# Odd high halves cast on VectorE instead of by DMA, and all squares on ScalarE

## The chip, the cores and the metric

The kernel runs on one core of one Trainium2 chip. The time is device microseconds of one execution; the kernel before took 1809.41 us (median of 3 runs, 1804.36 to 1811.67). Names used below: PE is TensorE's matmul side and PEld its weight loads, ACT is ScalarE, DVE is VectorE, POOL is GpSimd, SP is the sync engine, which here only issues DMAs.

## What is computed

An attention through 49 agents per batch, followed by a two-layer network with a squared ReLU between the layers:

```python
def _attn_ref(q, k, v, agents):
    scale = 1.0 / np.sqrt(q.shape[-1])
    def sm(a, b):
        s = scale * (a @ b.transpose(0, 2, 1))
        s = s - s.max(-1, keepdims=True)
        e = np.exp(s)
        return e / (e.sum(-1, keepdims=True) + 1e-09)
    agent_v = sm(agents, k) @ v
    return sm(q, agents) @ agent_v

def _moe_ref(x, w_in, w_out):
    h = x @ w_in
    r = np.maximum(h, 0.0)
    g = r * r
    return g @ w_out
```

There are 4 batches of 12480 rows with 128 channels; the network goes from 128 to 2048 hidden channels and back. All inputs are fp32.

## The kernel before

**Groups.** The 49920 rows are cut into 52 sets of 960 rows, and the 2048 hidden channels into 16 slices of 128. A set and a slice make a *group* i, from 0 to 831 (16 groups a set); g, gh, gl below are tiles of 128 hidden channels by 960 rows of one group. A group goes through these steps, in this order:

1. `mm1` on PE (L414): three pairs of matmuls give h in PSUM. The weights are agent values times w_in, and both operands are split in a rounded and a rest part (p_a, p_b, w_a, w_b). h has two buffers, so `mm1(i+2)` waits until `relu(i)` has read its h.
2. `relu` on ACT (L418), g from h.
3. `square` of g in place, on ACT (L424), or on DVE (L422) where `by_vector(i)` says so: from group 32 on, every fifth group (i % 5 == 3), 159 of 832.
4. `high`: gh, the rounded half of g, in the type that matmuls read at full rate. By a DMA from SBUF to SBUF that POOL issues (L429) for all groups but the last four, which DVE casts (L431).
5. `low` on DVE (L435): gl = g - gh, the rest.
6. `mm2` on PE (L453): two neighbouring groups j (even) and j+1 are taken together, gh of both with wo_hi and wo_lo, then gl of both with wo_hi. Within one call the order is: gh(j) with wo_hi, gh(j) with wo_lo, gh(j+1) with wo_hi, gh(j+1) with wo_lo, gl(j), gl(j+1). There are two calls for a pair, which differ in the halves of the PE array that the banks use.

**Order.** Every engine runs its instructions in the order in which the program issues them. The program collects all steps with a due time (`at(t, step)`), in units of one group, and sorts by it. `mm1(i)` is due at i, `relu(i)` at i + .1, `square(i)` at i + 1.2 (1.3 on DVE), `high(i)` at i + 3.05 by DMA and i + 2.35 on DVE, `low(i)` at i + 5.9 for even and i + 5.3 for odd groups with a DMA, i + 4.3 without one. The two `mm2` calls of the pair j, j+1 are due at j + 8 and j + 9 (LAG is 8). Due times set only the order; when a step runs is decided by its waits.

**Relay.** Between the two `mm2` calls of a pair the array's halves change places. A nop on POOL (L447) then waits for the matmuls before, and the matmuls after wait for the nop. So this nop stands in POOL's queue among the DMAs of `high`.

**Attention.** The work of the attention is put between the groups: scores of queries and keys on PE (L167), sums over values (L230), products for w_a and w_b (L310); exponentials on ACT (L209 for keys, L356 for queries), copies L182 and L319; maxima, sums, transposes and the store's copy (L469) on DVE. Its loads of kT, qT and v and the stores are issued by SP.

**Buffers.** g has 10, gh 9 and gl 7 buffers.

Of the kernel before, what the change touches and what calls it, by code (L numbers as in the profile page):

```python
# [13 lines left out]
AF = mybir.ActivationFunctionType  # L14
ALU = mybir.AluOpType
# [12 lines left out]
def agent_attention_relu2_kernel(ctx: ExitStack, tc: tile.TileContext, qT, kT, v, agT, w_in, w_out, outT):  # L28
# [6 lines left out]
    nc = tc.nc  # L35
# [4 lines left out]
    NF = F // P  # L40
    NSG = qT.shape[1] // ST
    NS = NSG // B
    NG = NSG * NF
# [350 lines left out]
    hs, gs, ghs, gls = {}, {}, {}, {}  # L394
# [23 lines left out]
        nc.scalar.activation(gs[i], hs.pop(i)[:, :, :TT], AF.Relu)  # L418

    def square(i):  # L420
        if by_vector(i):
            nc.vector.tensor_tensor(gs[i], gs[i], gs[i], op=ALU.mult)  # L422
        else:
            nc.scalar.activation(gs[i], gs[i], AF.Square)  # L424

    def high(i):
        ghs[i] = ew.tile([P, 2, TT], F32R, name="gh", bufs=HB)
        if by_dma(i):
            nc.gpsimd.dma_start(out=ghs[i], in_=gs[i])  # L429
        else:  # L430
            nc.vector.tensor_copy(ghs[i], gs[i])  # L431
# [47 lines left out]
    SKIP = (7, 12)  # L479

    def by_dma(i):
        return i < NG - 4

    def by_vector(i):
        return i >= 2 * NF and i % 5 == 3 and by_dma(i)

    steps = []

    def at(t, f, *args):
        steps.append((t, len(steps), f, args))  # L490
# [8 lines left out]
    def chain(t, todo):  # L499

        first = prev = None
        while todo:
            n = 1
            while todo[0][0] == "PE" and n < len(todo) and (todo[n][1] in reads_bank and todo[n][0] != "PE" or todo[n][1:-1] == todo[n - 1][1:-1] and todo[n][1] is not k_bias):
                n += 1
            t += hop[prev][todo[0][0]] if prev else 0
            while True:
                g, p, ts = t, None, []  # L510
                for e, f, *_ in todo[:n]:
                    g += hop[p][e] if p else 0
                    while (e, g) in taken:
                        g += 1
                    ts.append(g)
                    p = e
                held = range(ts[0], ts[-1] + (4 if todo[0][1] is v_acc else 2 if todo[0][1] is w_make else 3)) if todo[0][0] == "PE" else ()
                if not any(y in banks for y in held):
                    break
                t += 1  # L520
            banks.update(held)
            for (e, f, *args), g in zip(todo, ts):
                taken.add((e, g))
                at(g + (.005 + .015 * args[2] if f is w_make and args[2] < 2 else .5), f, *args)
            first = ts[0] if first is None else first
            prev, t, todo = p, ts[-1], todo[n:]
        return first, t
# [26 lines left out]
    def plan_keys(b, n, t):  # L554

        first, end = chain(t, [("PE", k_scores, b, n), ("ACT", k_copy, n), ("DVE", k_max, n)])
        for x in range(2):
            if b > 1 or n > 1:
                at(first - LEAD + .1 * x, k_load, b, 2 * n + x)
        print('K', b, n, first, end)  # L560
        return end

    def plan_bias(t):
        _, end = chain(t, [("DVE", k_bias, 0), ("PE", k_bias, 1), ("DVE", k_bias, 2), ("PE", k_bias, 3), ("DVE", k_bias, 4)])
        return end

    def plan_values(b, t0, stop):

        used, turned = {}, {}
        d = (stop - TAIL - t0) / NP  # L570
        for n in range(NP):
            _, t1 = turned[n] = chain(max(t0 + 1 + int(n * d), used.get(n - 2, 0)), [("ACT", k_exp, n), ("DVE", k_turn, n)])
            print('V', b, n, t1)
            used[n], end = chain(t1 + 3, [("PE", v_acc, n), ("DVE", v_sum, n)])
            for x in range(2):
                at(used[n] - LEAD + .1 * x, v_load, b, 2 * n + x)
        print('Vend', b, end, stop)
        last, end = chain(end + 2, [("PE", a_final, 0), ("DVE", a_final, 1), ("DVE", a_final, 2)])
        assert end < stop - 6, (b, end, stop)
        if b < B - 1:  # L580
            for n in range(NP):
                keys = plan_keys(b + 1, n, turned[n][1] + 5)
            return max(last + 2, plan_bias(keys + 1))
# [96 lines left out]
    for b in range(1, B):  # L680
        for f, x in enumerate((-6, -3, 0, 4)):
            first, end = chain(b * NS * NF + x, [("PE", w_make, b, f, 0), ("PX", w_make, b, f, 1), ("ACT", w_make, b, f, 2), ("DVE", w_make, b, f, 3)])
# [3 lines left out]
    end = 19  # L686
    for n in range(NP):
        end = plan_keys(1, n, end + 3)
    ready = plan_bias(end + 1)
    for b in range(1, B):  # L690
        ready = plan_values(b, ready, b * NS * NF)

    for i in range(NG):
        late = i in SKIP or i < NF + LAG and (i < LAG or (i - LAG) % NF == 0)
        at(i if late else i + .01, mm1, i)
        at(i + .1, relu, i)
        at(i + (1.3 if by_vector(i) else 1.2), square, i)
        if by_dma(i):
            at(i + 3.05, high, i)
            at(i + (5.3 if i % 2 else 5.9), low, i)  # L700
        else:
            at(i + 2.35, high, i)
            at(i + 4.3, low, i)
# [52 lines left out]
```

## Time and profile before

| | before |
|---|---|
| median of 3 runs | 1809.41 us |
| the profiled execution | 1806.67 us |
| its span, first to last instruction | 1804.9 us |
| busy: PE, DVE, ACT, POOL | 1748.7, 1449.7, 1471.4, 477.7 us |
| DMA queues: packets' share of 16 engines, software and hardware queue | 68.7% and 21.3% |
| moved by the 828 DMAs gh<-g, 480 KB each | 4.7 us median from issue to landing |

The span is 1.8 us shorter than the time of the same execution. A matmul's end in the profile is modelled, and neighbouring matmuls overlap, so a busy share of 97% for PE doesn't mean that the array lost only 3%. Of the waits, only what stands between two instructions of one engine is shown, with the event that ended it.

### The profile page before, as it was taken

The numbers are of one execution on the slowest core, as the hardware profiler recorded it, in microseconds if no ns is written. First come the engines' busy times: TensorE is split into PE (matmuls) and PEld (weight loads), VectorE is DVE, ScalarE is ACT, GpSimd is POOL, SyncE is SP. The second block draws the span as 40 slices with busy tenths as digits, with TensorE's granted clock in tenths as the row PEclk, the third lists the DMA queues.
The fourth block names the chain that finished last, engine by engine and source line by source line (L and its number), as shares of the span: only waits on it lengthen the run. The fifth ranks groups of instructions, "written<-read, shape, count | busy, mean of one in ns | idle before, by whom it ended". The sixth has DMA issues, their size and how long they took to land.

```text
span 1804.9 us, 41518 instructions
## 1 busy us (share of the span) xinstructions
PE 1748.7 (97%) x16831; PEld 1493.8 (83%) x16835; DVE 1449.7 (80%) x1509; ACT 1471.4 (82%) x1645; POOL 477.7 (26%) x897
## 2 busy tenths in 40 slices
PE   8899999999999999999999999999999999999998
PEld 4578787888887887888888888888898898889897
DVE  6978777787886886787887787887888789788886
ACT  4788877887887887888888788887898898889886
POOL 0322222222222222222222222222232222223231
PEclk9999999999999999999999999999999999999999
DMA  9799998999989989989979889989998998999885
GB/s 375 263 302 350 302 275 305 308 318 318 304 271 347 293 292 311 316 283 336 306 274 306 262 308 320 303 277 307 297 294 277 299 307 294 303 302 305 289 303 193
DMA packets 169664, 541.42 MB, mean 300 GB/s; under 512 B 21806, under 2 KB 34368, under 8 KB 169472
## 3 DMA queue, kind: packets, MB, share of 16 engines
q0 software_dynamic: 127136, 419.18, 68.7%
q1 hardware_dynamic: 42336, 119.59, 21.3%
q8 instruction: 132, 2.16, 0.5%
q14 instruction: 60, 0.49, 0.1%
HBM read 81.47 MB, written 25.56 MB: 59 GB/s over the span
## 4 chain that ended last, share of the span: by engine, by line
PE 68%; DMA 17%; issue 6%; DVE 4%; ACT 3%; POOL 0%; SPq 0%; POOLq 0%; DVEq 0%; ACTq 0%
PE out L453 41%; PE h L414 20%; DMA gh<-g 16%; PE ps_att L167 4%; ACT g L424 3%; DVE gl L435 3%; PE ps_att L230 1%; DMA kt<-kT 1%; PE ps_att L310 1%; PE out L230 0%; ACT g L418 0%; DVE g L422 0%; DVE cv_x L88 0%; POOL wo_lo L113 0%; PE h L167 0%
## 5 line engine op out<-in xcount | busy, mean ns | idle before, releaser
L435 DVE TENSOR_TENSOR gl<-g,gh 128x960 fp32r<-128x960 f32 x832 | 934.3, 1149 | 242.1 <-DMA gh<-g 208.8
L418 ACT ACTIVATE g<-h 128x960 f32<-128x960 f32 x832 | 807.7, 971 | 286.2 <-PE h L414 282.9
L429 POOL DMA_DIRECT2D gh<-g x828 | 439.5, 531 | 1243.3 <-ACT g L424 724.5
L424 ACT ACTIVATE g<-g 128x960 f32<-128x960 f32 x673 | 670.7, 997 | 0.0
L453 PE MATMUL out<-gh,wo_hi 64*128 64x480 f32 x3328 | 627.5, 373 | 25.5 <-DMA gh<-g 16.7
L453 PE MATMUL out<-gh,wo_lo 64*128 64x480 f32 x3328 | 610.4, 363 | 0.0
L453 PE MATMUL out<-gl,wo_hi 64*128 64x480 f32 x3328 | 490.8, 368 | 15.7 <-DVE gl L435 15.2
L453 PEld LDWEIGHTS out<-gh,wo_hi 64*128 64x128 f32 x3328 | 314.3, 185 | 106.7 <-issue 38.9
L453 PEld LDWEIGHTS out<-gl,wo_hi 64*128 64x128 f32 x3328 | 316.8, 187 | 57.4 <-DVE gl L435 35.4
L453 PEld LDWEIGHTS out<-gh,wo_lo 64*128 64x128 f32 x3328 | 317.5, 187 | 21.2
L414 PE MATMUL h<-p_a,w_a 49*128 49x480 f32 x1664 | 311.5, 371 | 0.5 <-ACT w_a L294 0.4
L414 PE MATMUL h<-p_a,w_b 49*128 49x480 f32 x1664 | 305.4, 363 | 0.0
L414 PE MATMUL h<-p_b,w_a 49*128 49x480 f32 x1664 | 304.9, 363 | 0.0
L422 DVE TENSOR_TENSOR g<-g 128x960 f32<-128x960 f32 x159 | 183.0, 1151 | 29.2 <-ACT g L418 28.2
L414 PEld LDWEIGHTS h<-p_a,w_a 49*128 49x128 f32 x1664 | 158.9, 187 | 15.4 <-ACT g L418 2.9
L414 PEld LDWEIGHTS h<-p_b,w_a 49*128 49x128 f32 x1664 | 160.4, 189 | 10.9
L414 PEld LDWEIGHTS h<-p_a,w_b 49*128 49x128 f32 x1664 | 157.0, 185 | 12.8
L469 DVE COPY ob<-out 128x960 f32<-128x960 f32 x51 | 58.7, 1151 | 14.5 <-PE out L453 14.2
L167 PE MATMUL ps_att<-qt,ag_sb 128*32 128x480 f32 x408 | 47.2, 572 | 0.7 <-DVE w_b L321 0.7
L344 DVE STREAM_TRANSPOSE e<-ps_att 128x960 f32<-128x960 f32 (+1 forms) x26 | 30.7, 1179 | 10.8 <-PE ps_att L167 10.5
L230 PE MATMUL ps_att<-vt,pe 128*49 128x129 f32 x588 | 36.7, 275 | 0.0
L230 PEld LDWEIGHTS ps_att<-vt,pe 128*49 128x49 f32 x588 | 31.4, 123 | 6.4 <-issue 5.2
(95 smaller groups left out, 596.8 us busy)
## 6 DMA issues: line engine op xcount, KB each, us to landing
gh<-g POOLq DMA_DIRECT2D x828, 480.0 KB, 4.7
vt<-v SPq DMA_DIRECT2D x56, 451.5 KB, 9.0
kt<-kT SPq DMA_DIRECT2D x56, 448.0 KB, 8.3
qt<-qT SPq DMA_DIRECT2D x52, 480.0 KB, 7.0
outT<-ob SPq DMA_DIRECT2D x51, 480.0 KB, 5.2
pt<-et SPq DMA_DIRECT2D x204, 60.0 KB, 5.8
p_a<-pt POOLq DMA_DIRECT2D x50, 211.9 KB, 3.8
raw<-w_in SPq DMA_DIRECT2D x4, 512.0 KB, 10.7
```

The lines of the kernel that those rows point to most:

```text
L167: nc.tensor.matmul(ps[32 * j:32 * j + 32, h, :w], ags[j // 2][:, 32 * h:32 * h + 32], xs[j // 2][:, j % 2 * w:j % 2 * w + w], start=True, ...
L230: nc.tensor.matmul(ps[t:t + A, :C + 1], pes[n][:, c, :A], vt[:, y, :], start=n == first and c < 2, stop=n == last and c >= KC - 2)
L310: mm = nc.tensor.matmul(ps[:M, u, :256], av2[rows], win_sb[rows, f * 512 + u * 256:f * 512 + u * 256 + 256], start=step == 0, stop=step == 1)
L344: nc.vector.transpose(squares(es[u]), pss.pop(("q", u))[r, :, :TT].rearrange("p h (b c) -> p h b c", c=32))
L414: nc.tensor.matmul(hs[i][:, t, :TT], w, two(p), start=n == 0, stop=n == 2)
L418: nc.scalar.activation(gs[i], hs.pop(i)[:, :, :TT], AF.Relu)
L422: nc.vector.tensor_tensor(gs[i], gs[i], gs[i], op=ALU.mult)
L424: nc.scalar.activation(gs[i], gs[i], AF.Square)
L429: nc.gpsimd.dma_start(out=ghs[i], in_=gs[i])
L435: nc.vector.tensor_tensor(out=gls[i], in0=gs.pop(i), in1=ghs[i].bitcast(F32), op=ALU.subtract)
L453: mm = nc.tensor.matmul(o[:, u, :TT], w[rows, j, :], two(g[rows, u, :]), start=first and n == 0, stop=last and n == len(todo) - 1)
L469: nc.vector.tensor_copy(ob, o[:, :, :TT])
```

## The change

From group 48 on (the fourth set of 16), odd groups no longer get gh by DMA: DVE casts them, due at i + 2.35, and their `low` is due at i + 4.3. That is 390 of the 828 DMAs. Even groups keep the DMA. `by_vector` goes, so that the 159 squares of DVE run on ACT, due at i + 1.2. Two lines that only print are dropped.

```diff
     def square(i):
-        if by_vector(i):
-            nc.vector.tensor_tensor(gs[i], gs[i], gs[i], op=ALU.mult)
-        else:
-            nc.scalar.activation(gs[i], gs[i], AF.Square)
+        nc.scalar.activation(gs[i], gs[i], AF.Square)
...
     def by_dma(i):
-        return i < NG - 4
-
-    def by_vector(i):
-        return i >= 2 * NF and i % 5 == 3 and by_dma(i)
+        return i < NG - 4 and (i % 2 == 0 or i < 3 * NF)
...
         at(i + .1, relu, i)
-        at(i + (1.3 if by_vector(i) else 1.2), square, i)
+        at(i + 1.2, square, i)
         if by_dma(i):
             at(i + 3.05, high, i)
             at(i + (5.3 if i % 2 else 5.9), low, i)
```

(In the lines below these, `else` gives a group without a DMA its cast at i + 2.35 and its `low` at i + 4.3, as before.) Line numbers of `high`, `low`, `mm2` and `store` are smaller by 3 after the change, and `square` is L421.

DVE's queue before, at groups 98 to 103. Here g_3456 belongs to group 98, g_3483 to 99, g_3509 to 100, g_3547 to 101, g_3573 to 102 and g_3606 to 103:

```order
L435 TENSOR_TENSOR gl_3615<-g_3456,gh_3545 128x960
L435 TENSOR_TENSOR gl_3641<-g_3483,gh_3571 128x960
L422 TENSOR_TENSOR g_3606<-g_3606 128x960
L352 TENSOR_TENSOR e_3523<-e_3523,mx_3578 128x15x49
L435 TENSOR_TENSOR gl_3672<-g_3509,gh_3602 128x960
L435 TENSOR_TENSOR gl_3698<-g_3547,gh_3637 128x960
L391 TENSOR_TENSOR p_b_3610<-pt_3239,p_a_3609 113x480
L213 STREAM_TRANSPOSE pe_3730<-sk_87 128x2x14x32
L435 TENSOR_TENSOR gl_3732<-g_3573,gh_3664 128x960
```

The same place after it. Here g_3458 belongs to group 98, g_3483 to 99, g_3511 to 100, g_3547 to 101, g_3606 to 103 and g_3666 to 105:

```order
L432 TENSOR_TENSOR gl_3609<-g_3483,gh_3552 128x960
L428 CAST gh_3611<-g_3547 128x960
L466 COPY ob_3616<-out_3122 128x960
L432 TENSOR_TENSOR gl_3619<-g_3458,gh_3545 128x960
L432 TENSOR_TENSOR gl_3669<-g_3547,gh_3611 128x960
L428 CAST gh_3671<-g_3606 128x960
L352 TENSOR_TENSOR e_3523<-e_3523,mx_3578 128x15x49
L432 TENSOR_TENSOR gl_3676<-g_3511,gh_3602 128x960
L391 TENSOR_TENSOR p_b_3614<-pt_3243,p_a_3613 113x480
L432 TENSOR_TENSOR gl_3730<-g_3606,gh_3671 128x960
L428 CAST gh_3732<-g_3666 128x960
L213 STREAM_TRANSPOSE pe_3734<-sk_87 128x2x14x32
```

The subtraction of an odd group (101) has moved ahead of that of its even neighbour (100), a cast of the next odd group stands behind each of them, and the square of group 103 is gone from this queue.

ACT's queue before, at the square that DVE has (group 98, g_3456):

```order
L418 ACTIVATE g_3456<-h_3447 128x960
L424 ACTIVATE g_3430<-g_3430 128x960
L418 ACTIVATE g_3483<-h_3474 128x960
L418 ACTIVATE g_3509<-h_3500 128x960
L424 ACTIVATE g_3483<-g_3483 128x960
```

And after it (group 98 is g_3458):

```order
L418 ACTIVATE g_3458<-h_3451 128x960
L421 ACTIVATE g_3430<-g_3430 128x960
L418 ACTIVATE g_3483<-h_3474 128x960
L421 ACTIVATE g_3458<-g_3458 128x960
L418 ACTIVATE g_3511<-h_3504 128x960
L421 ACTIVATE g_3483<-g_3483 128x960
```

Before, two ReLUs stood side by side in every fifth group; now a square stands between any two of them. In both, the square of a group comes behind the ReLU of the next one.

## Rows read from the trace of the kernel before

**Rows 1.** The page: busy time of each engine, share of the span, instructions.
```profile
PE 1748.7 (97%) x16831; PEld 1493.8 (83%) x16835; DVE 1449.7 (80%) x1509; ACT 1471.4 (82%) x1645; POOL 477.7 (26%) x897
```
**Rows 2.** The page: costliest groups (busy us, mean ns of one, idle before, releaser).
```profile
L418 ACT ACTIVATE g<-h 128x960 f32<-128x960 f32 x832 | 807.7, 971 | 286.2 <-PE h L414 282.9
...
L424 ACT ACTIVATE g<-g 128x960 f32<-128x960 f32 x673 | 670.7, 997 | 0.0
...
L422 DVE TENSOR_TENSOR g<-g 128x960 f32<-128x960 f32 x159 | 183.0, 1151 | 29.2 <-ACT g L418 28.2
```
**Rows 3.** The page: the chain that ended last, by engine.
```profile
PE 68%; DMA 17%; issue 6%; DVE 4%; ACT 3%; POOL 0%; SPq 0%; POOLq 0%; DVEq 0%; ACTq 0%
```
**Rows 4.** Waits of PE from 160 to 1786 us: us in total, times, longest.
```profile
PE out L453 <- DMA gh<-g: 16.7, 19, 2.5
PE out L453 <- DVE gl L435: 12.0, 33, 0.5
PE out L453 <- POOLq L447: 5.6, 12, 0.5
```
**Rows 5.** Waits of DVE and of ACT, the same stretch.
```profile
DVE gl L435 <- DMA gh<-g: 201.6, 170, 4.2
DVE g L422 <- ACT g L418: 27.5, 31, 2.5
...
ACT g L418 <- PE h L414: 269.1, 252, 4.1
```
**Rows 6.** Timeline, 286 to 302 us: start, length, instruction, [idle before it, releaser].
```profile
287.83 1.53 SPq L175 DMA_DIRECT2D kt<-kT  x2
...
289.47 1.35 SPq L219 DMA_DIRECT2D vt<-v  x2
...
294.13 0.36 PE L453 MATMUL out<-gh,wo_lo 64*128 64x480 f32 x2
...
296.10 1.16 DVE L435 TENSOR_TENSOR gl<-g,gh 128x960 fp32r<-128x960 f32 x1 [3.63 <-DMA gh<-g]
296.12 0.47 PE L453 MATMUL out<-gh,wo_hi 64*128 64x480 f32 x2 [1.63 <-DMA gh<-g]
```
**Rows 7.** Clock: the whole span, and windows behind stalls (PEclk stands ahead of DMA share).
```profile
core 0: 1804.9 us, clock 0.992
...
297.50:301.00 3.50, 3.50 (x20) 2.96 (x20) 2.51 (x3) 1.95 (x3) 0.53 (x1) 0.52 1.10 408
1024.00:1031.00 7.00, 6.60 (x36) 5.11 (x38) 6.99 (x7) 2.03 (x3) 1.59 (x3) 0.55 0.66 213
```
**Rows 8.** Window 160 to 1786 us: busy time of each engine, clock, DMA share, GB/s.
```profile
160.00:1786.00 1626.00, 1591.24 (x15442) 1384.87 (x15440) 1316.32 (x1345) 1352.67 (x1503) 440.21 (x830) 0.99 0.91 300
```
**Rows 9.** Timeline of ACT behind an exponential, and of ACT and PE undisturbed.
```profile
902.17 0.95 ACT L418 ACTIVATE g<-h 128x960 f32<-128x960 f32 x1
...
903.91 0.96 ACT L418 ACTIVATE g<-h 128x960 f32<-128x960 f32 x1
...
908.51 0.37 PE L414 MATMUL h<-p_a,w_a 49*128 49x480 f32 x2
...
909.33 0.97 ACT L418 ACTIVATE g<-h 128x960 f32<-128x960 f32 x1 [0.86 <-PE h L414]
...
910.34 0.37 PE L414 MATMUL h<-p_a,w_a 49*128 49x480 f32 x2
```
**Rows 10.** The four casts of the tail, by line; tile gh, issue to landing of its DMAs.
```profile
L431 DVE CAST gh<-g 128x960 fp32r<-128x960 f32 x4 | 2.6, 654 | 1.2 <-ACT g L424 1.2
...
DMA to landing us min/median/max: 2.8/4.7/10.8
```
**Rows 11.** Attention's exponentials on ACT, 160 to 1786 us, by line.
```profile
L209 ACT ACTIVATE sk<-sk,mb 128x448 f32<-128x448 f32 x42 | 25.5, 658 | 0.0
L356 ACT ACTIVATE e<-e 128x735 f32<-128x735 f32 (+1 forms) x23 | 18.9, 822 | 0.0
```
**Rows 12.** Tile gh, POOL's issues (ns min/median/max); timeline at 80 us, POOL and DVE.
```profile
L429 POOL DMA_DIRECT2D gh<-g x828: 527/530/1085, 56.4 to 1785.6; - x166
...
80.60 1.60 POOL L429 DMA_DIRECT2D gh<-g  x2
80.76 0.45 DVE L85 TENSOR_SCALAR cv_p<-sk 128x512 uint32<-128x512 uint32 x1
81.10 0.47 DVE L87 TENSOR_SCALAR cv_x<-sk 128x512 uint32<-128x512 uint32 x1
```

More of the change, by code (lines that the diff above doesn't have):

```diff
@@ L559, in plan_keys @@
                 at(first - LEAD + .1 * x, k_load, b, 2 * n + x)
-        print('K', b, n, first, end)
         return end
@@ L572, in plan_values @@
             _, t1 = turned[n] = chain(max(t0 + 1 + int(n * d), used.get(n - 2, 0)), [("ACT", k_exp, n), ("DVE", k_turn, n)])
-            print('V', b, n, t1)
             used[n], end = chain(t1 + 3, [("PE", v_acc, n), ("DVE", v_sum, n)])
@@ L576, in plan_values @@
                 at(used[n] - LEAD + .1 * x, v_load, b, 2 * n + x)
-        print('Vend', b, end, stop)
         last, end = chain(end + 2, [("PE", a_final, 0), ("DVE", a_final, 1), ("DVE", a_final, 2)])
```

## The prediction

> **What bounds the kernel now.** The share of busy time comes first: PE is busy for 97% of the span, ACT for 82%, DVE for 80% [rows 1]. So PE is the engine to feed, and the most that a change to the other engines can give back is PE's stalls. The chain that ended last runs through PE for 68% and through DMA for 17% [rows 3], which says that the DMA of gh often arrives last, not that 17% can be saved. The waits of PE tell how much: from 160 to 1786 us it idles 16.7 us for the DMA of gh (19 times), 12.0 us for gl from DVE (33 times) and 5.6 us for the relay nop on POOL (12 times), 34.3 us in all [rows 4]. Since a matmul's end is modelled, a stall is a little longer than its idle time. A unit (one group) undisturbed takes 910.34 - 908.51 = 1.83 us [rows 9] for nine pairs of matmuls, 0.20 us each; in the stall at 296 us the starts are 1.99 us apart, 1.79 us more than 0.20, where the row says 1.63 [rows 6]. That is 0.15 us more per stall.
>
> That stall also shows the mechanism. The matmul that waits is gh with wo_hi right behind gh with wo_lo, so it is the second, odd group of the pair. Four big loads (two kt, two vt) were issued 5 to 8 us before and share the DMA engines, which are 91% busy [rows 6, 8]. The DMA of gh takes 4.7 us in the median, but 2.8 at best and 10.8 at worst [rows 10]. DVE had then stood for 3.63 us for the same DMA [rows 6]; over the stretch it stands 201.6 us that way [rows 5]. Behind the worst stalls PE's granted clock falls to its lower level, 1.2 GHz: 0.52 and 0.55 of full speed in two such windows [rows 7].
>
> **What is removed.** Four terms, against the profiled execution's 1806.67 us.
>
> Waits for gh: 16.7 + 19 x 0.15 = 19.6 us. The odd group's gh now comes from a cast that is due 4.65 units (8.5 us) before `mm2` needs it, and the even group's DMA runs in a queue that lost 390 of 828 transfers. I take all of it: 19.6.
>
> Waits for gl: 12.0 + 33 x 0.15 = 17.0 us. Gl is late because DVE was held by a DMA, or because DVE is simply behind. The first cause falls away for odd groups and becomes rarer for even ones; the second stays. I take two thirds: 11.3.
>
> Waits for the relay: 5.6 + 12 x 0.15 = 7.4 us. The nop stands in POOL's queue right behind the DMA of an odd group, which waits for that group's square. With odd groups gone, the DMA ahead of the nop is an even one, due two units before it instead of one. I take 7.4.
>
> Clock: 0.008 of the span is missing from full speed [rows 7], 14.4 us, a part of it at the start and the end. I take 10 us as the stalls' share and 8 as what goes with them.
>
> Sum: 46 us.
>
> **What is added, and what hides it.** On DVE, 390 casts at the tail's 654 ns [rows 10] are 255 us, and 159 squares at 1151 ns less [rows 2] are 183 us: 72 us more work, 1522 us, 84% of the span. DVE has 310 us idle in the stretch, 201.6 of it waits for the DMA of gh [rows 5, 8]; the work fits if these waits shrink. On the path I count nothing: within a pair DVE does a cast and two subtractions, and the gl that is done last is due more than 2 units before its matmul. If that cover is gone, every further wait of DVE is gl late at PE.
>
> A cast puts a wait in DVE's queue: for the square on ACT. Behind it are queued the subtraction of the even group and everything of the attention. The nearest row is the square on DVE that goes away, which waited for ACT in the same way: 27.5 us for 156 of them in the stretch [rows 5], 0.18 us each; the four casts of the tail waited 1.2 us together, 0.3 each [rows 10]. So 70 to 117 us for 390 casts, below the 201.6 us of DMA waits that they replace in part. I take nothing on the path, between a gain of some us (DVE is freer) and the loss under the second rival.
>
> On ACT, 159 squares at 997 ns [rows 2] are 159 us: 1630 us busy, 90% of the span. Idle time that it takes: 269.1 us of waiting for h [rows 5]. Undisturbed, ACT waits for PE in every unit; behind an exponential, two ReLUs start 1.74 us apart [rows 9], against PE's 1.83. So ACT keeps pace with squares in every unit but makes up only 0.09 us per unit. A ReLU starts 0.82 us after its `mm1` and lasts 0.97 [rows 9]; `mm1` two units on, 3.65 us later, needs it, so ACT may be 1.8 us late at no cost. An exponential of keys (two of 0.66) makes it 1.3 us late, one of queries 0.8 [rows 11]; both together pass the limit, and attention work on PE gives the time back. Bounds: nothing, and all exponentials of the stretch, 25.5 + 18.9 = 44 us [rows 11]. Most should be absorbed: I take 8.
>
> On POOL, 390 issues of 0.53 us go. Casts and issues can meet: one issue of 828 took 1.085 us instead of 0.53, while two one-input operations of DVE ran, of the kind that the cast is [rows 12]. That bounds the price at 0 and 0.55 us per DMA; an even group's DMA has more than that before DVE needs it, so I take nothing.
> The Trainium skill is harsher here (SBUF — State Buffer, "A bandwidth-pool intuition that's wrong"): a DMA issued by GpSimd that takes about 620 ns alone takes about 3100 ns when a VectorE `tensor_copy` overlaps it, since descriptors can't be written meanwhile. By that page an even group's DMA would be about 2.5 us late where it meets a cast, and the sum, as an estimate, would be the time of now, with nothing gained. No row here shows a delay of that size; the largest is the 0.55 us, and the sum goes by that.
>
> Sum: 1806.67 - 46 + 8 = 1768.7 us. The median of the runs is 2.7 us above the profiled execution, so I predict **1771 us**.
>
> **The rivals.**
>
> *The stalls move to the even groups.* The even group's gh still comes by DMA, its subtraction now stands behind a cast and an odd subtraction, and loads still come in bursts. Then the gl waits stay, half the gh waits too, and half the clock's loss: 46 - 11 - 10 - 4 = 21 gained, less 4 on ACT: 1792 us. For it: even and odd DMAs were equally slow in the queue. Against: the odd one was last each time, and the queue becomes shorter.
>
> *ACT becomes the bound.* ACT regains only 0.09 us a unit, so every exponential is paid in full: 44 us instead of 8 [rows 11]: 1807 us, no change. Against: attention's work on PE is spread over the same units, and ACT idles 269 us now [rows 5].
>
> *The casts hold POOL's issues.* If every one of the 390 casts meets an issue and delays it by 0.55 us, and the subtraction behind it waits that much longer, DVE is held for 215 us, as long as by DMAs now (201.6 us [rows 5]), and the four terms stay: 1806.67 + 2.7 = 1809 us. For it: the 1.085 us issue [rows 12]. Against: the median of 828 issues is 0.53. The Trainium skill's page above is this rival at a higher price.
>
> *Slower: DVE is held at the casts.* DVE's queue is strict, and a cast stands where its square is only just done. In the stretch DVE would work 1316 - 180 + 255 = 1391 of 1626 us [rows 2, 8, 10], and has other waits of 310 - 202 - 28 = 80 us [rows 5, 8]. That leaves 155 us, 0.4 us per cast. From an average wait of 0.4 us on, DVE sets the time. At 0.5 us it would be 390 x 0.1 = 39 us longer than now: 1848 us. Against: 0.18 and 0.3 us in the nearest rows, and a wait of this kind falls away as soon as DVE is behind.
>
> **How the numbers follow.** The forecast has 0.55, the even groups 0.15, ACT 0.13, POOL's collisions 0.05, DVE held at the casts 0.12. Faster or slower by over 0.5% (9 us) is about what a measurement of this kernel can tell from no change. The forecast and the first rival are faster (0.70), ACT and POOL are the same (0.18), the last is slower (0.12). The forecast's own range reaches from 1755 (all 54 us of the four terms gone, nothing added) to 1790 (half the gain). The range must also take in the first two rivals and the third: 1752 to 1810.
>
> **What would show each step.** PE's waits for the DMA of gh all but gone from its list, the relay's too, and the waits for gl at a third. The granted clock without windows at 1.2 GHz in the middle. The DMA gh<-g below 4 us in the median, the DMA engines below 70%. Casts of 0.65 us; a wait "cast for the square on ACT" of about 0.2 us each; DVE's waits for the DMA below 70 us. ACT at 90 to 92%, with PE's `mm1` waiting for a ReLU only now and then. The prediction is wrong if `mm1` waits for ACT regularly, if issues on POOL or casts get much longer than 0.53 and 0.65 us, or if DVE's wait for ACT at the casts is above 0.4 us on average while gl is what PE waits for.

## The result and the profile after

The changed kernel takes **1739.39 us** (median of 4 runs, 1735.89 to 1739.94) beside 1810.54 us of the kernel before (4 runs): ratio 0.9603, 95% interval 0.9568 to 0.9638, so 3.6 to 4.3% faster. The sign and the mechanism were forecast, the size was not: 1771 us was predicted, and the measured time lies below the range's 1752 us. The profiled execution took 1735.89 us, 70.8 us less than that of before; the sum had 38.

The page of the changed kernel: busy time by engine; the chain that ended last; the costliest groups that answer to [rows 2, 10].

```profile
PE 1713.3 (99%) x16831; PEld 1499.6 (86%) x16835; DVE 1488.7 (86%) x1740; ACT 1594.3 (92%) x1804; POOL 271.4 (16%) x507
...
PE 94%; DMA 2%; DVE 2%; ACT 1%; issue 1%; SPq 0%; DVEq 0%; ACTq 0%; POOLq 0%
...
L432 DVE TENSOR_TENSOR gl<-g,gh 128x960 fp32r<-128x960 f32 x832 | 933.6, 1147 | 39.8 <-DMA gh<-g 36.1
L418 ACT ACTIVATE g<-h 128x960 f32<-128x960 f32 x832 | 811.1, 975 | 97.2 <-PE h L414 97.0
L421 ACT ACTIVATE g<-g 128x960 f32<-128x960 f32 x832 | 835.5, 1004 | 0.0
...
L428 DVE CAST gh<-g 128x960 fp32r<-128x960 f32 x394 | 258.6, 656 | 123.7 <-ACT g L421 123.1
```

The chain now runs through PE for 94% of the span; the DMA's 17% [rows 3] have become 2%. The next rows are the waits of PE, DVE and ACT from 155 or 160 us to the end of the steady part (engine, line, who was waited for: us, times, longest), the answer to [rows 4, 5]; then the clock of the whole span and the busy times from 160 to 1710 us, the answer to [rows 7, 8].

```profile
PE out L450 <- DVE gl L432: 0.2, 1, 0.2
...
DVE gh L428 <- ACT g L421: 122.3, 146, 2.1
DVE e L344 <- PE ps_att L167: 34.8, 22, 1.8
DVE gl L432 <- DMA gh<-g: 20.7, 21, 2.3
...
ACT g L418 <- PE h L414: 86.7, 75, 1.9
...
core 0: 1734.0 us, clock 1.000
...
160.00:1710.00 1550.00, 1549.81 (x15346) 1383.70 (x15344) 1353.71 (x1569) 1463.75 (x1648) 231.88 (x437) 1.00 0.58 190
```

PE idles 0.2 us in 1550 where it idled 34.3 [rows 4]. No wait for a DMA, none for the relay, none for ScalarE is left; the clock stays at its upper level. DVE's wait for the DMA of gh fell from 201.6 to 20.7 us. Between the first matmul of group 48 and that of group 831 lie 1561.0 us, before 1627.5. So 66.5 of the 70.8 us come from the steady part, where PE's stalls were, and 4.3 from the start and the end of the kernel. Of these 4.3 the change can't be said to have earned 3.4: group 48 begins at 160.7 us before and at 157.3 after, but at 160.1 in the kernel 'casts due later' below, which has the same steps as the changed kernel up to there. The granted clock from 20 to 100 us was 0.96 in the profiles of the kernel before and of 'casts due later', and 1.00 in that of the changed kernel.

### The profile page after: what moved, and what is told of

Read it like the earlier page. It is cut to its first block, busy times and chain, and to the rows that moved or that the text cites. A ratio compares the mean times of both kernels' runs of the same rounds, so it can differ in the third digit from the quotient of the medians.

```text
span 1734.0 us, 41600 instructions
## 1 busy us (share of the span) xinstructions
PE 1713.3 (99%) x16831; PEld 1499.6 (86%) x16835; DVE 1488.7 (86%) x1740; ACT 1594.3 (92%) x1804; POOL 271.4 (16%) x507
## 4 chain that ended last, share of the span: by engine, by line
PE 94%; DMA 2%; DVE 2%; ACT 1%; issue 1%; SPq 0%; DVEq 0%; ACTq 0%; POOLq 0%
PE out L450 58%; PE h L414 28%; PE ps_att L167 4%; PE ps_att L230 2%; DMA kt<-kT 1%; DMA gh<-g 1%; PE ps_att L310 1%; DVE gl L432 1%; PE out L230 0%; DMA qt<-qT 0%; ACT g L421 0%; SPq L175 0%; DVE pe L213 0%; ACT g L418 0%; DVE mx L348 0%
## 5 line engine op out<-in xcount | busy, mean ns | idle before, releaser
L421 ACT ACTIVATE g<-g 128x960 f32<-128x960 f32 x832 | 835.5, 1004 | 0.0
L450 PE MATMUL out<-gl,wo_hi 64*128 64x480 f32 x3328 | 477.4, 363 | 3.3 <-DVE gl L432 3.1
L426 POOL DMA_DIRECT2D gh<-g x438 | 232.4, 531 | 1379.7 <-ACT g L421 668.0
L428 DVE CAST gh<-g 128x960 fp32r<-128x960 f32 x394 | 258.6, 656 | 123.7 <-ACT g L421 123.1
L209 ACT ACTIVATE sk<-sk,mb 128x448 f32<-128x448 f32 x56 | 33.9, 664 | 3.1 <-DVE mb L205 3.1
```

Source lines behind the costliest of these rows:

```text
L209: nc.scalar.activation(sk[:, n, h], sk[:, n, h], AF.Exp, bias=mb[:, h:h + 1], scale=scale)
L450: mm = nc.tensor.matmul(o[:, u, :TT], w[rows, j, :], two(g[rows, u, :]), start=first and n == 0, stop=last and n == len(todo) - 1)
```

## The experiments

Three questions: which of the two parts does it; is it the shorter DMA queue or the odd group's place in it; and why the gain is nearly twice the sum. The kernel before was timed anew beside each series, at 1809 to 1811 us. The kernels are listed with their medians, and from their profiles from 160 to 1710 us the DMA engines' share, the median from issue to landing of gh's DMA (whole run), and PE's idle time (1550 us less its busy time).

| kernel | us | above the changed one | DMA share | gh landing | PE idle |
|---|---|---|---|---|---|
| before | 1810.5 | 71 | 0.92 | 4.7 | 34.5 |
| changed | 1739.4 | | 0.58 | 3.6 | 0.2 |
| casts only | 1766.0 | 27 | 0.57 | 3.4 | 15.3 |
| squares only | 1807.5 | 68 | 0.92 | 4.8 | 34.8 |
| DMA load back | 1749.5 | 10 | 0.86 | 4.6 | 7.7 |
| every fourth group cast | 1773.5 | 34 | 0.75 | 3.8 | 18.5 |
| even groups cast | 1753.0 | 14 | 0.57 | 3.1 | 9.0 |
| even groups cast, load back | 1783.7 | 44 | 0.84 | 4.4 | 22.5 |
| casts due later | 1741.6 | 2 | 0.58 | 3.4 | 1.0 |
| more on ScalarE | 1763.5 | 24 | 0.57 | 3.2 | 8.1 |
| casts from group 16 | 1736.5 | -3 | 0.57 | 3.5 | 0.2 |

### One part alone

Casts only, `square` as before (`by_vector` and the due time i + 1.3 come back with it; only the main lines of an edit are shown):

```diff
     def square(i):
-        nc.scalar.activation(gs[i], gs[i], AF.Square)
+        if by_vector(i):
+            nc.vector.tensor_tensor(gs[i], gs[i], gs[i], op=ALU.mult)
+        else:
+            nc.scalar.activation(gs[i], gs[i], AF.Square)
```

> The casts of odd groups on VectorE as in the changed kernel, but every fifth square stays on VectorE. VectorE then has 1488.7 + 183 = 1672 us of work, 96% of a span of 1740. Theory 'both parts are needed' (the squares make room on VectorE for the casts): VectorE falls behind, PE waits for gl again, 1765 to 1810 us. Theory 'only the DMAs matter': PE stays free of waits, 1740 us within 6.

Squares only:

```diff
     def by_dma(i):
-        return i < NG - 4 and (i % 2 == 0 or i < 3 * NF)
+        return i < NG - 4
```

> All squares on ScalarE, but gh of all groups up to 827 by DMA, as before. The DMA engines stay at 90% busy. Theory 'the DMA of gh is what PE waited for': the waits for gh stay, at best those for gl shrink, 1785 to 1812 us. Theory 'VectorE was behind, and its 183 us of squares were the cause': half of the 71 us or more is gained, 1740 to 1775 us.

The casts alone took 1765.96 us (ratio 0.9764, 0.973 to 0.9799), the squares alone 1807.50 (0.9984, 0.9965 to 1.0004: no difference). Busy times and PE's waits, first of the kernel with casts only, then of the kernel with squares only:

```profile
PE 1727.6 (98%) x16835; PEld 1491.4 (85%) x16835; DVE 1645.4 (93%) x1899; ACT 1468.5 (83%) x1645; POOL 275.7 (16%) x507
...
PE out L453 <- DVE gl L435: 14.2, 22, 1.4
PE out L453 <- DMA gh<-g: 0.2, 1, 0.2
```
```profile
PE 1747.9 (97%) x16835; PEld 1495.2 (83%) x16835; DVE 1287.7 (71%) x1350; ACT 1599.4 (89%) x1804; POOL 476.8 (26%) x897
...
PE out L450 <- DMA gh<-g: 21.4, 21, 3.1
PE out L450 <- DVE gl L432: 12.1, 31, 0.4
...
PE out L450 <- POOLq L444: 0.3, 1, 0.3
```

With the casts and every fifth square on DVE, it is busy for 93% and has become what PE waits for; the DMA of gh is all but gone from the list (0.2 us). With squares on ScalarE and no casts, DVE is busy for 1287.7 us instead of 1449.7, and PE waits for gh and gl as before; only the wait for the relay is gone, and the one for gh has grown by nearly as much. So the casts carry the gain, the squares alone are worth nothing, and behind the casts they are worth 27 us, since they make room for them on DVE.

### The queue or the place

Load on the DMA engines brought back, and nothing that waits for it (the copies have no use):

```diff
+    def extra(i):
+        part = win_sb[:, i // 2 % 2 * ST:(i // 2 % 2 + 1) * ST]
+        nc.gpsimd.dma_start(out=part, in_=part)
...
             at(i + 2.35, high, i)
+            if i < NG - 4 and 12 <= i % (NS * NF) < 190:
+                at(i + 3.05, extra, i)
```

> The changed kernel, with 338 DMAs of 480 KB each from SBUF onto itself (no use for the result), issued by GpSimd where the odd groups' DMAs stood. Nothing waits for them but the next of them, so only their load on the DMA engines is back (share about 85%). Theory 'queue': what helped is the shorter queue, so loads and the even groups' gh are late again, VectorE waits for them, 1765 to 1800 us. Theory 'place': what helped is that the odd group, whose gl had the least slack, no longer hangs on a DMA at all, 1739 to 1750 us.

Every fourth group cast:

```diff
-        return i < NG - 4 and (i % 2 == 0 or i < 3 * NF)
+        return i < NG - 4 and (i % 4 != 1 or i < 3 * NF)
```

> All squares on ScalarE, but only every fourth group (i % 4 == 1, 195 of them) is cast on VectorE; the DMA engines' share falls to about 75% instead of 58%. Theory 'queue': the spare share grows from 9% to 25%, most of the gain is there, 1740 to 1755 us. Theory 'place': half of the odd groups still hang on a DMA, half of the gain, 1765 to 1785 us.

Even groups cast instead of odd ones:

```diff
-        return i < NG - 4 and (i % 2 == 0 or i < 3 * NF)
+        return i < NG - 4 and (i % 2 == 1 or i < 3 * NF)
```

> As the changed kernel, but from group 48 on the even groups are cast on VectorE and the odd ones keep the DMA: the same number of DMAs (438), casts and instructions on each engine. Theory 'place': the odd group has less time between its square and its matmul, and its DMA is what PE waited for; PE waits for gh and gl again, though less than before, since the queue is shorter: 1755 to 1790 us. Theory 'number': any 390 DMAs fewer would do: 1739 us within 8.

And this edit together with the load of the first:

> The even groups are cast on VectorE, the odd ones keep the DMA, and 338 DMAs of 480 KB from SBUF onto itself (without use for the result) bring the load on the DMA engines back to about 85%. Each half of this alone cost little (odd groups on the DMA in a short queue 14 us, the full load with the odd groups cast 10 us). Theory 'both must come together': the loss is far above 14 + 10, PE waits for gh and gl as in the kernel before, 1785 to 1810 us. Theory 'the two add up': 1755 to 1772 us.

Measured: 1749.45 us (0.9668, 0.9623 to 0.9712), 1773.53 (0.98, 0.9762 to 0.9837), 1752.98 (0.9678, 0.9641 to 0.9715) and 1783.73 (0.9848, 0.9814 to 0.9883). For the four kernels in this order, the waits of PE for gh and gl and of DVE for the DMA, 160 to 1710 us (for the first also PE's wait for a load of q):

```profile
PE ps_att L167 <- DMA qt<-qT: 6.2, 3, 3.0
PE out L450 <- DVE gl L432: 1.3, 3, 0.7
...
DVE gl L432 <- DMA gh<-g: 50.6, 50, 2.6
```
```profile
PE out L450 <- DMA gh<-g: 9.6, 10, 2.4
PE out L450 <- DVE gl L432: 7.3, 20, 0.5
...
DVE gl L432 <- DMA gh<-g: 85.3, 59, 3.6
```
```profile
PE out L450 <- DMA gh<-g: 4.3, 5, 1.5
PE out L450 <- DVE gl L432: 4.0, 10, 0.8
...
DVE gl L432 <- DMA gh<-g: 145.6, 93, 5.6
```
```profile
PE out L450 <- DMA gh<-g: 12.9, 13, 2.0
PE out L450 <- DVE gl L432: 9.1, 27, 0.4
...
DVE gl L432 <- DMA gh<-g: 198.9, 124, 4.5
```

With the full load back (share 0.86, gh's DMA as slow as before) and the odd groups cast, PE still doesn't wait for gh, and only 10 us are lost, as theory 'place' had it. Most of that is a load of q that came late: 6.2 of PE's 7.7 us of idle time in that profile. Every fourth group cast also lies where 'place' had it. So the shorter queue alone is not it. But with the odd groups on the DMA in the short queue only 14 us are lost, less than 'place' and more than 'number' had expected, so the odd group's place alone isn't it either. Both together lose 44 us, where 10 and 14 would add up to 24. The theory that both must come together expected 1785 or more and is met almost; the sum of the two is off by 11 us and more.

What the place means can be read from the plan: an odd group's `high` is due as late after its `mm1` as an even one's, but its matmul comes 7 units after it instead of 8, and its DMA stands behind the even one's. So the odd one has 1.8 us less to spare, and in a queue that is 92% full a DMA of gh took up to 10.8 us, where the median is 4.7 [rows 10]. PE's order in the traces bears this out: before, 18 of the 19 waits for gh and all 33 for gl [rows 4] stand at the matmul of the odd group, and so do all waits for gh in the last three of these four kernels. That 27 us still lie between the last kernel and the one before is not explained: there the even groups hang on the DMA too and the share is 0.92, and which of the two matters was not tried. The squares, which differ as well, are worth nothing alone.

### Margins of DVE and ScalarE

Casts due later:

```diff
-            at(i + 2.35, high, i)
+            at(i + (3.05 if i < NG - 4 else 2.35), high, i)
```

> As the changed kernel, but a cast is due at i + 3.05 instead of i + 2.35, so that it stands behind one more subtraction in VectorE's queue. In the changed kernel VectorE waits 122 us at the casts for the square on ScalarE. Theory 'these waits cost nothing, since PE has no wait left': waits at the casts fall below 60 us, the time stays, 1739 us within 6. Theory 'VectorE is near its limit and the waits are paid': 5 to 15 us faster, 1724 to 1734 us.

A second activation in every eighth group:

```diff
         nc.scalar.activation(gs[i], gs[i], AF.Square)
+        if 3 * NF <= i < NG - 4 and i % EVERY == 0:
+            nc.scalar.activation(gs[i], gs[i], AF.Relu)
...
+    EVERY = 8
```

> As the changed kernel, with a second activation (a ReLU of the square, which changes nothing) in every eighth group from 48 on: 98 more on ScalarE at 0.87 to 1.0 us, 85 to 98 us, so 97% busy. In the changed kernel ScalarE waits 87 us for h. Theory 'lateness up to 1.8 us is free and the idle time can be used': 1739 to 1755 us. Theory 'ScalarE is the next bound, since its idle time lies beside the attention's work on PE and cannot be used': the 85 us are paid nearly in full, 1795 to 1825 us.

Casts from the second set on:

```diff
-        return i < NG - 4 and (i % 2 == 0 or i < 3 * NF)
+        return i < NG - 4 and (i % 2 == 0 or i < NF)
```

> As the changed kernel, but odd groups are cast on VectorE from group 16 on instead of 48, 16 more casts while the conversion of the weights still runs on VectorE. From 85 to 157 us the changed kernel has stalls of about 2 us on PE. Theory 'the DMA is the cause there too': 1 to 3 us faster. Theory 'VectorE is full there': 2 to 10 us slower.

Casts due later took 1741.58 us (0.9617, 0.9583 to 0.965), no clear difference from the changed kernel. DVE's waits there:

```profile
DVE gl L432 <- DMA gh<-g: 50.7, 39, 4.4
DVE e L344 <- PE ps_att L167: 42.2, 19, 2.9
...
DVE gh L428 <- ACT g L421: 11.5, 23, 0.7
```

The wait at the casts fell from 122 to 11.5 us and came back in part at other places of DVE's queue. Since PE hardly waits for DVE (0.7 us here), neither is paid: the 122 us were DVE's spare time.

More work on ScalarE took 1763.53 us (0.9741, 0.9701 to 0.9781), 24 us for 98 activations, between the two theories. ScalarE's added group (98.5 us busy) and PE's waits:

```profile
L423 ACT ACTIVATE g<-g 128x960 f32<-128x960 f32 x98 | 98.5, 1005 | 3.1
...
PE h L414 <- ACT g L418: 4.8, 12, 0.9
PE out L452 <- DVE gl L434: 1.5, 4, 0.5
```

Now PE does wait for a ReLU (12 times), and 4 times for gl; what made gl late is not shown. These rows hold 6 of the 24 us. Compared matmul by matmul with the changed kernel, as is done for the stalls below, 11.6 us more lie in distances for which no wait is listed. So ScalarE's margin is real but small: at 92% busy nothing is lost, at 95% a quarter of the added work is.

Casts from the second set took 1736.49 us (0.9591, 0.9557 to 0.9626), the fastest median, but its interval overlaps nearly all of the changed kernel's, and from group 48 to 831 it takes the same 1561.0 us; that it is faster isn't shown.

## Why the prediction was right in direction and wrong in size

**The waits for gh, taken in full: right.** The second, odd group was what PE waited for (18 of 19 times), and its cast ended that; the experiments on the place confirm the step, with the addition that it hurts much less in a short queue (14 us). The row of PE's waits for gh is empty, so the stalls did not move to the even groups either.

**The waits for gl, two thirds taken: too little.** All but 0.2 us went. DVE was thought to be behind by itself in a third of the cases. But in 30 of the 33 cases before, DVE had stood for a DMA of gh at one of its last seven instructions up to the late subtraction, and with squares only, where DVE had 162 us less to do, PE waited for gl as before. So DVE was late through the DMA. With 86% of the span busy and hardly a DMA to wait for it is in time; 5.7 us of the miss.

**The relay, taken in full: right in size, the reason only in part.** The prediction put it down to the odd group's DMA right ahead of the nop, which waits for that group's square. In 11 of the 12 cases before, that square was one of those on DVE. With squares only, the odd groups' DMAs still stand ahead of the nop, and 0.3 us are left of the wait. So it was the DMAs that waited for a square on DVE, and either half of the change ends that.

**The price of a stall, its idle time and 0.15 us: the step that failed.** The four terms came to 54 us if all of it went, so that 1755 us was the best that its terms could give; the steady part gave back 66.5. The 0.15 us were about right. What the sum put at nothing is the first matmul behind a stall, and the delays for which no wait is listed. The same stall of before shows what the row of idle time leaves out, in the starts of the matmuls that follow it (timeline of PE, before):

```profile
296.43 0.37 PE L453 MATMUL out<-gh,wo_lo 64*128 64x480 f32 x2
296.63 0.36 PE L453 MATMUL out<-gl,wo_hi 64*128 64x480 f32 x2
297.31 0.50 PE L453 MATMUL out<-gl,wo_hi 64*128 64x480 f32 x2 [0.32 <-DVE gl L435]
297.62 0.59 PE L414 MATMUL h<-p_a,w_a 49*128 49x480 f32 x2
298.00 0.61 PE L414 MATMUL h<-p_b,w_a 49*128 49x480 f32 x2
298.40 0.61 PE L414 MATMUL h<-p_a,w_b 49*128 49x480 f32 x2
```

The matmul after a stall starts at 296.12 [rows 6] and the next one at 296.43, 0.31 us later instead of 0.20: the stall costs 0.11 us once more when it ends. Then gl stalls at 297.31: 0.68 us after 296.63, so 0.48 too much, with 0.32 of idle time in the row. From 297.62 on the starts are 0.38 to 0.40 us apart, the lower clock. PE has the same matmuls in the same order in both kernels, so the distances between starts can be compared one by one, from the first matmul of group 48 to that of group 831, where the two kernels differ by 66.5 us. The 64 distances with a wait of [rows 4] were 45.0 us longer before than in the changed kernel; the sum has 34.3 + 64 x 0.15 = 43.9 for them. The 64 distances right behind them were 7.0 us longer (61 of them lasted 0.31 us), the others at the lower clock 9.0, where the sum has 8, and all the rest 5.4: delays too short to be listed as a wait, and the matmuls behind them. So the stalls and the clock were about right, and the restart (7.0 us) and the unlisted delays (5.4 us) were not in the sum.

**ScalarE, 8 us on the path: too much.** It is the largest single item of the miss. PE's list has no wait for a ReLU, so nothing was paid. That the lateness of 1.8 us is free and the exponentials are made up fits; the added activations show that the margin ends soon after.

**DVE at the casts: right.** 122.3 us for 389 casts in the stretch are 0.31 us each, just above the 0.18 to 0.3 that were expected and below the 0.4 from which DVE would set the time. **The casts' length: right**, 656 ns against 654.

**Casts and POOL's issues: right to take nothing.** In the changed kernel the two hardly meet: 5 of the 438 issues overlap a cast. With the casts due later 166 do; there an issue took 997 ns at the longest, and 528 in the median (tile gh, min/median/max, of that kernel):

```profile
L426 POOL DMA_DIRECT2D gh<-g x389: 527/528/997, 161.2 to 1707.0; - x195
L428 DVE CAST gh<-g x387: 639/653/758, 167.8 to 1710.0; 128x960 fp32r<-128x960 f32 x194
```

So a collision cost up to 0.47 us on POOL and 0.1 on DVE, within the bound of 0.55 and far from the 2.5 us of the prediction's harsher estimate, and the time stayed.

What is left of the miss are 4.3 us at the start and the end, which the sum took as unchanged, and which come in the main from the executions that were profiled. Summed up: 38.3 predicted, 5.7 for gl, 8 for ScalarE, 7.0 for the restarts, 5.4 for the unlisted delays, 1.1 for the stalls themselves, 1.0 for the clock and 4.3 at the ends give the 70.8.

## What to carry to other kernels

The idle time of PE between matmuls is a lower bound of what its stalls cost: by the table, a us of idle time stood for 1.5 to 2.1 us of run time in the kernels here that were held by gh or gl, and for 3 in the one with more on ScalarE. The distance between the starts of matmuls is the better measure. When a step has its transfers in a full queue, look which of its instances has the least slack: taking the odd groups off the queue won 14 us more than taking as many even ones off. And a second change that gains nothing alone can be what makes room for the first.

## What was not expected of the hardware

After a stall of 1.8 us on PE and one of 0.5 us that followed it, PE ran for 3.5 us at a granted clock of 0.52, that is mostly at 1.2 GHz [rows 6, 7]. The length of one stall alone does not tell: before, the clock from 834 to 841 us, from a stall of 1.5 us of idle time on, was 1.00, and from 1191.9 to 1195.3 us, behind three stalls of 0.4 to 0.5 us, 0.50. The first pair of matmuls after a stall took 0.31 us to the next instead of 0.20 in 61 of 64 cases. In the changed kernel the first pair behind a matmul of the attention took the same 0.31 us about 70 times, with no wait listed. A DMA from SBUF to SBUF of 480 KB landed 4.7 us after its issue in the median at a DMA share of 0.92 and 3.1 to 3.6 us at 0.57 to 0.58, with 2.8 us at best in every kernel.
